# Attention beside a feed-forward network: one head in four forms its scores once, and a transfer turns its probabilities

## The chip, the cores and the metric

One core of one Trainium2 chip. The time is device microseconds of one execution of the whole program; the comparison is between medians of several runs.

## The reference, cut to what matters

`x` is 2048 × 448, there are 16 heads of 28 columns, and the sequence is cut into 4 segments of 512. Within a segment each head attends causally; between segments a linear memory is carried. A feed-forward network runs on the same `x`, and a gate mixes both.

```python
g = sigmoid((x * gate_w).sum(-1, keepdims=True))
# attention, per segment s and head:
logits = einsum("bhqd,bhkd->bhqk", qs, ks) * scale + mask      # causal, 512 x 512
a_dot  = einsum("bhqk,bhkd->bhqd", softmax(logits), vs)
a_mem  = (phi(qs) @ M) / (phi(qs) @ z + 1e-6)                   # memory of earlier segments
o      = sigmoid(beta) * a_mem + (1 - sigmoid(beta)) * a_dot
M, z   = M + phi(ks)^T vs, z + phi(ks) summed
a = concat(o) @ wo
b = silu(x @ w1) @ w2                                           # 448 -> 1792 -> 448
out = g * a + (1 - g) * b
```

## The kernel before, in words

All products run in 16-bit halves: a number is split into a high half and the low half that is left, and a product is the sum of three products of halves. The high half is a copy on ScalarE (ACT), the low half a subtract on VectorE (DVE) or GpSimd (POOL).

The program has three stages. **Projections** (`project`): the features `xT`, the weights `wqs`, `wks`, `wvs`, and from them q, k and v of all segments, which go to DRAM (`q_scr`, `k_scr`, `v_scr`), and the memory terms. `xquarter` (L769) splits the first segment's features in four pieces on DVE (L783, L784), and `weight` (L811) splits the weights (L822; for wq and wk on DVE or POOL, whichever the planner finds free first). `size` (L387) takes largest magnitudes, `scales` (L413 to L431) makes powers of two from them; its TensorE transpose (L417) waits for `most`.

**Attention, with the first FFN pass between.** The 64 heads are taken in 16 groups of four, t = 0 to 15. For each group `maxima(t)` loads q and k into one of four buffers (`ring`), forms all causal scores with queries on partitions (L668; the first block of the four heads shares one bank, which L664 first fills with the mask), and takes row maxima (L673, L678, with the mask tile `mk` added). The maxima go through a small transpose (L686) and two steps (L688, L692) to DRAM (`m_scr`) and come back as two more rows of q. `attention(t)` then forms the scores a second time, now with keys on partitions and the maximum as part of the product (L1219, contraction over 86 rows), in three banks: 512 columns, 384 + 128, 256. ACT takes the exponentials into `pf` (L1224); POOL clears the triangle on the diagonal blocks (L1227, L1230); ACT writes the high half into `phl` (L1236), POOL the low half in three pieces (L1240). With keys on partitions, `phl` is at once the left operand of the product with v (PV, L1253: 20 small products for a head), and DVE adds up its two halves (L1261). Around it run the FFN: the first product (L563, `xh` × `wa`), tanh and the halves (L1098 to L1104), the second product (L1121). Each segment's 16-bit features `xh` are made by `x16` from loads into the two buffers `rawf`.

**The end**: the second FFN pass with the output projection. Its inputs `oT` come by transposing transfers (L588, DMA_TRANSPOSE, 7 blocks of 128 × 128 each).

What sets the order: every instruction group is a task with a priority (`prio`; a head has 10, a group 40), planned durations (`half`, `act`, `dve`, `pool`, `dma`) and buffers. `Sched` plays the program forward and, engine by engine, emits the task that can start first, and among those the one of the least priority. The result is one fixed instruction list for each engine; an engine then waits at each instruction for what it needs. All transfers are issued from SyncE's (SP's) one list. Constants such as `MAXO`, `LOP`, `PVP`, `FLO`, `FHI` shift priorities.

Of the kernel before, what the change touches and what calls it, by code (L numbers as in the profile page):

```python
# [8 lines left out]
F32 = mybir.dt.float32  # L9
# [12 lines left out]
KS = 3 * DH  # L22
# [8 lines left out]
NEG = -1.0e30  # L31
NT = NSEG * NG
NH = NT * 4
NA = 5
COLD = 5.0
# [10 lines left out]
WOT = 59.67  # L46
# [5 lines left out]
HD = 0.15  # L52
# [3 lines left out]
LOP = 11.21  # L56
# [3 lines left out]
MAXO = 66.73  # L60
# [9 lines left out]
VC = -7.68  # L70
OT1 = 8.22
XS = 6.38
QS = -4.77
KS1 = 0.43
# [7 lines left out]
PRICE = 34.19  # L82
PVRUNS = [((1, 0), 1)]
PVP = 44.58
FLO = -16.6
FHI = 688.88
WOP = 89.36
# [27 lines left out]
class Sched:  # L115
# [6 lines left out]
    def __init__(self):  # L122
        self.free = {e: 1.0 for e in self.HOP}
        self.cand = {e: [] for e in self.HOP}
        self.count = 0
        self.port = {"DVE": 0.0, "POOL": 0.0}
        self.tail = 1.0
# [116 lines left out]
def infini_mix(ctx: ExitStack, tc: tile.TileContext, x, wq, wk, wv, wo, beta, w1, w2, out):  # L244
# [226 lines left out]
    def others(s, prio, bds, own, t_own, t_gh):  # L471
# [15 lines left out]
        def scores():  # L487
# [3 lines left out]
            nc.vector.reciprocal(lift[:, s:s + 1], es[:, s:s + 1])  # L491
            nc.vector.tensor_scalar(lift[:, s:s + 1], lift[:, s:s + 1], LIFT, 2.0 ** 29, op0=OP.mult, op1=OP.min)
# [140 lines left out]
    cring("mx", [128, 4, TB], F32, 2, base)  # L633
    cring("mhl2", [16, 2, 128], F16, 1, base)
# [9 lines left out]
    def maxima(t, o):  # L644
# [9 lines left out]
        RDONE[:] = RS[t] = rs  # L654
        reds = []
        plan = [(0, [0, 1, 2, 3]), (1, [0, 1]), (1, [2, 3])] + [(i, [h]) for h in range(4) for i in (2, 3)]
        for q, (i, hs) in enumerate(plan):
# [4 lines left out]
            def go(i=i, hs=hs, ps=ps, n=n):  # L662
                if i == 0:
                    nc.tensor.matmul(ps.v, identb, maskb[:, None, :].to_broadcast([128, 4, 128]), start=True,  # L664
                                     stop=False, skip_group_check=True)
                for j, hh in enumerate(hs):
                    u = j * n
                    nc.tensor.matmul(ps.v[:, u:u + n], rg.v[:KS, 0, hh, i * 128:(i + 1) * 128], rg.v[:KS, 1, hh, :n],  # L668
                                     start=(i > 0), stop=(i > 0 or j == 3), skip_group_check=(i == 0))

            def red(i=i, hs=hs, ps=ps, n=n):
                if i == 0:
                    nc.vector.tensor_reduce(mx.v[:, :, 0], ps.v.rearrange("p (h n) -> p h n", h=4), axis=AX.X,  # L673
                                            op=OP.max)
                    return
# [4 lines left out]
            m = pe((half(512) if i == 0 else []) + half(n, len(hs)), go, *rs, *MKS, takes=[ps], uses=[rg], prio=p0)  # L680
# [5 lines left out]
        f0 = pe(half(128), lambda: nc.tensor.transpose(pt.v[:16, :128], mx.v.rearrange("p h i -> p (h i)"), ident), *reds,  # L686
                takes=[pt], uses=[mx], prio=p0)
        f1 = dve(128, lambda: nc.vector.tensor_scalar(pt.v[:16, :128], pt.v[:16, :128], lift[:16, s:s + 1], None,  # L688
                                                      op0=OP.subtract), f0, EREADY[s], uses=[pt], prio=p0)
        f3 = act(128, lambda: nc.scalar.activation(mh.v[:, 0], pt.v[:16, :128], AF.Copy, scale=1.0 / TALL), f1, takes=[mh],  # L690
                 uses=[pt], prio=p0)
        f4 = dve(128, lambda: nc.vector.scalar_tensor_tensor(mh.v[:, 1], pt.v[:16, :128], 1.0 / TALL, mh.v[:, 0],  # L692
                                                             op0=OP.mult, op1=OP.subtract), f3, uses=[pt, mh], prio=p0)
        d1 = dma(16e3, lambda: start(mscr[t].rearrange("z h i n -> (h i) z n"), mh.v), f4, uses=[mh], prio=p0)
        dm = dma(16e3, lambda: start(rg.v[KS:KS + 2, 0], mscr[t].rearrange("z h i n -> z h (i n)")), d1, uses=[rg],
# [3 lines left out]
    def project():  # L699
# [110 lines left out]

        def weight(name, src, prio, places):  # L811
            n = W[name].shape[2]
            for c, (b, first, v) in enumerate(places):
# [16 lines left out]
                WS[name][c] = [hi, dve(n, lambda lo=lo: lo(nc.vector), hi, **k) if name == "v" else either(n, lo, hi, **k)]  # L830
# [243 lines left out]
    TH, GF, PA = (tiles(fp, n, [128, L], F32, 2) for n in ("th", "gf", "pa"))  # L1074
# [68 lines left out]
    def spare(s, p0, m):  # L1143
        th, gf, g = Buf(TH), Buf(GF), Buf(GTR)
        if s not in SP:
# [4 lines left out]
        e2 = dve(L, lambda: nc.vector.scalar_tensor_tensor(gf.v, th.v, 1.0, h.v, op0=OP.add, op1=OP.mult), e1,  # L1150
                 port=True, takes=[gf], uses=[h, th], prio=p0)
# [257 lines left out]
```

## Time and profile before

| | us |
|---|---|
| median of 3 runs | 558.12 (557.57 to 558.83) |
| the profiled execution | 557.23 |
| its span (first to last instruction) | 555.5 |
| TensorE busy | 541.9 |
| VectorE busy | 413.6 |
| ScalarE busy | 399.7 |
| GpSimd busy | 365.2 |

In the profile, a group is a line of the kernel with its engine, operation and tile names (out<-in), so `L1224 ACT ACTIVATE pf<-sc,es` is the exponential. Its columns are the busy time of all, the mean of one in ns, and the idle time of the engine just before them with what ended it. TensorE's weight loads have a row of their own (PEld) and run beside the products. `SPq` is SyncE's list of transfers: its times are those of the issue, not of the data.

### The profile page before, as it was taken

The numbers are of one execution on the slowest core, as the hardware profiler recorded it, in microseconds if no ns is written. First come the engines' busy times: TensorE is split into PE (matmuls) and PEld (weight loads), VectorE is DVE, ScalarE is ACT, GpSimd is POOL, SyncE is SP. The second block draws the span as 40 slices with busy tenths as digits, with TensorE's granted clock in tenths as the row PEclk, the third lists the DMA queues.
The fourth block names the chain that finished last, engine by engine and source line by source line (L and its number), as shares of the span: only waits on it lengthen the run. The fifth ranks groups of instructions, "written<-read, shape, count | busy, mean of one in ns | idle before, by whom it ended". The sixth has DMA issues, their size and how long they took to land.

```text
span 555.5 us, 11580 instructions
## 1 busy us (share of the span) xinstructions
PE 541.9 (98%) x4007; PEld 340.2 (61%) x4007; DVE 413.6 (74%) x1076; ACT 399.7 (72%) x695; POOL 365.2 (66%) x520
## 2 busy tenths in 40 slices
PE   8799999999999999999999999999999999999997
PEld 5588888888844555555656545565556555555544
DVE  6997998788789966789656888857997228745463
ACT  6467988876656878899778978878998897403140
POOL 5813648637320777999899979998999996212220
PEclk9899999999999999999999999999999999999999
DMA  8479888986775445423344235357302213689972
GB/s 293 153 241 217 229 220 242 224 213 188 216 211 163 130 136 176 122 74 79 108 118 127 68 88 155 108 139 180 90 19 70 69 50 94 226 208 222 251 183 83
DMA packets 91497, 85.87 MB, mean 155 GB/s; under 512 B 55432, under 2 KB 79112, under 8 KB 91440
## 3 DMA queue, kind: packets, MB, share of 16 engines
q1 hardware_dynamic: 91440, 85.15, 55.6%
q8 instruction: 31, 0.51, 0.4%
q14 instruction: 26, 0.21, 0.1%
HBM read 52.60 MB, written 26.09 MB: 142 GB/s over the span
## 4 chain that ended last, share of the span: by engine, by line
PE 84%; POOL 5%; DVE 4%; ACT 3%; DMA 2%; issue 2%; DVEq 0%; POOLq 0%; ACTq 0%
PE mm L563 32%; PE mm L1121 22%; PE sc L563 11%; PE sc L668 5%; PE sc L1219 5%; PE cc L1253 5%; POOL phl L1240 3%; DMA rawf<-in_x_dram 1%; ACT pf L1224 1%; PE cc L973 1%; ACT phl L1236 1%; DVE sizes L387 1%; PE cc L936 1%; DMA xraw<-in_x_dram 1%; PE cc L974 1%
## 5 line engine op out<-in xcount | busy, mean ns | idle before, releaser
L1240 POOL TENSOR_TENSOR phl<-pf,phl 128x384 f16<-128x384 f32 (+1 forms) x192 | 189.2, 1004 | 14.9 <-ACT phl L1236 14.8
L1121 PE MATMUL mm<-wb,ghl 128*128 128x448 f16 (+1 forms) x684 | 148.2, 349 | 0.0
L563 PE MATMUL mm<-xh,wa 128*128 128x512 f16 x572 | 140.3, 379 | 0.0
L1224 ACT ACTIVATE pf<-sc,es 128x512 f32<-128x512 f32 (+1 forms) x192 | 109.6, 620 | 15.7 <-PE sc L1219 12.6
L678 DVE CUSTOM_DVE_ANT_0 sc<-sc,mk 128x384 f32<-128x384 f32 (+1 forms) x192 | 104.6, 572 | 18.0 <-PE sc L668 16.6
L1121 PEld LDWEIGHTS <-ghl 128*128 128x128 f16 x684 | 64.7, 97 | 51.7 <-issue 1.0
L1236 ACT ACTIVATE phl<-pf 128x1280 f16<-128x1280 f32 x64 | 81.4, 1274 | 12.4 <-POOL pf L1230 12.3
L563 PEld LDWEIGHTS <-wa 128*128 128x128 f16 x572 | 53.6, 97 | 53.8 <-issue 0.3
L1219 PE MATMUL sc<-ring 86*128 86x512 f16 (+3 forms) x256 | 58.3, 299 | 2.2 <-ACT pf L1224 1.8
L668 PE MATMUL sc<-ring 84*128 84x128 f16 (+3 forms) x256 | 56.1, 299 | 0.5 <-ACT pf L1224 0.5
L1253 PEld LDWEIGHTS <-phl 128*128 128x128 f16 x1280 | 41.9, 96 | 8.8
L574 POOL TENSOR_TENSOR ol<-ol,ml 128x448 f32<-128x448 f32 x12 | 13.6, 1133 | 51.1 <-DMA ol<-o_scr 42.0
L563 PE MATMUL mm<-xT,wqs 128*128 128x512 f32 x176 | 47.2, 406 | 0.0
L563 PE MATMUL mm<-xT,wks 128*128 128x512 f32 x176 | 45.9, 400 | 0.0
L1098 ACT ACTIVATE th<-mm,ths 128x512 f32<-128x512 f32 x52 | 35.5, 689 | 13.3 <-PE mm L563 13.2
L1253 PE MATMUL cc<-vg,phl 128*128 128x29 f16 (+1 forms) x1280 | 43.6, 182 | 0.0
L1261 DVE TENSOR_REDUCE oraw<-cc 128x116 f32<-128x232 f32 x64 | 25.1, 393 | 23.3 <-PE cc L1253 23.1
L563 PE MATMUL sc<-wvs,xT 128*128 128x450 f32 x176 | 40.4, 373 | 1.0 <-DVE wvs L822 1.0
L1219 PEld LDWEIGHTS <-ring 86*128 86x128 f16 x256 | 24.5, 97 | 26.3 <-issue 3.5
L1227 POOL TENSOR_SCALAR_AFFINE_SELECT pf<-pf 128x128 f32<-128x128 f32 x64 | 20.9, 326 | 27.7 <-ACT pf L1224 25.3
L1104 DVE SCALAR_TENSOR_TENSOR ghl<-mm,ghl 128x512 f16<-128x512 f32 x52 | 35.1, 680 | 5.2 <-ACT ghl L1102 5.1
L1100 DVE SCALAR_TENSOR_TENSOR mm<-th,mm 128x512 f32<-128x512 f32 x52 | 35.4, 691 | 4.1 <-ACT th L1098 4.0
(162 smaller groups left out, 912.1 us busy)
## 6 DMA issues: line engine op xcount, KB each, us to landing
rawf<-in_w_dram SPq DMA_DIRECT2D x26, 256.0 KB
rawf<-in_w_dram SPq DMA_DIRECT2D x28, 224.0 KB
xraw<-in_x_dram SPq DMA_DIRECT2D x16, 256.0 KB
rawf<-in_x_dram SPq DMA_DIRECT2D x16, 256.0 KB
v_scr<-vt SPq DMA_DIRECT2D x16, 232.0 KB
vg<-v_scr SPq DMA_DIRECT2D x16, 232.0 KB
q_scr<-stg SPq DMA_DIRECT2D x16, 224.0 KB
k_scr<-stg SPq DMA_DIRECT2D x16, 224.0 KB
```

The source lines that it names most:

```text
L563: nc.tensor.matmul(ps(), *p[i], start=(i == 0), stop=(i == n - 1))
L668: nc.tensor.matmul(ps.v[:, u:u + n], rg.v[:KS, 0, hh, i * 128:(i + 1) * 128], rg.v[:KS, 1, hh, :n], start=(i > 0), stop=(i > 0 or j == 3), ...
L678: nc.vector.tensor_tensor_reduce(r, r, MK[:, L - n:], 1.0, NEG, OP.add, OP.max, mx.v[:, hh, i:i + 1])
L1098: e1 = sact(L, lambda ps=ps, th=th: nc.scalar.activation(th.v, ps.v, AF.Tanh, scale=ths[:, s:s + 1]), m, takes=[th], uses=[ps], prio=p0)
L1100: e2 = dve(L, lambda ps=ps, th=th: nc.vector.scalar_tensor_tensor(ps.v, th.v, 1.0, ps.v, op0=OP.add, op1=OP.mult), e1, uses=[ps, th], prio=p0)
L1104: e4 = dve(L, lambda ps=ps, g=g: nc.vector.scalar_tensor_tensor(g.v[:, 1], ps.v, DOWN, g.v[:, 0], op0=OP.mult, op1=OP.subtract), e3, uses= ...
L1121: nc.tensor.matmul(ps.v[:, lo:hi], g.v[:, y, sl], w.v[:, z, lo:hi], start=(j == 0 and i == 0), stop=(j == len(fs) - 1 and i == 2))
L1219: nc.tensor.matmul(ps.v[:, e:e + w], rg.v[:KK, 1, hh, j * 128:(j + 1) * 128], rg.v[:KK, 0, hh, j * 128:], start=True, stop=True)
L1224: ex.append(sact(e, lambda b=b, ps=ps, pf=pf, e=e: nc.scalar.activation(pf.v[:, b, :e], ps.v[:, :e], AF.Exp, scale=es[:, s:s + 1]), m, *ex ...
L1236: hi = copy(1280, lambda hl=hl, flat=flat: nc.scalar.activation(hl.v[:, 0], flat(), AF.Copy), *mk, takes=[hl], uses=[pf], prio=p0 + 2)
L1240: low = pool(w - u, lambda hl=hl, flat=flat, u=u, w=w: nc.gpsimd.tensor_sub(hl.v[:, 1, u:w], flat()[:, u:w], hl.v[:, 0, u:w]), low, uses=[ ...
L1253: nc.tensor.matmul(p[:, i, :2 - z], hl.v[:, z, u:u + 128], vg.v[:, j, hh, :2 - z], start=(z == zs[0] and i == 0), stop=(z == zs[-1] and j ...
```

## The change

For groups 1 to 15 the last head is "turned" (`TURNED`). Its scores are formed once, with queries on partitions (4 products, contraction over 84 rows), in three banks: block 3 (512 columns), blocks 2 and 0 (384 + 128), block 1 (256). DVE adds the mask and takes the row maximum, and four one-column operations make the exponential's bias. ACT takes four exponentials with that bias and then the high half, POOL the low half. The probabilities now have queries on partitions, so a transposing transfer turns both halves, 20 blocks of 128 × 128, from `phl` back into the memory of `pf`, and PV reads them from there. `maxima` forms and sends three heads' maxima instead of four for these groups, and the two selects on POOL are not needed for the turned head.

Besides, `pf` has four buffers instead of three, and `gf` goes (its values overwrite `hsum`). In the projections, the low halves of wq and wk also wait for the low halves of the first segment's features (`XLO`). Some fifteen priority constants have other values.

```diff
+NPF = 4
+NPH = 3
+TURNED = [0] + [1] * 15
+TQ = 31.32
+TPV = 38.99
+TD = 3.4
+TDLAT = 4.0
...
-FHI = 688.88
+FHI = 674.33
...
+            nc.vector.tensor_scalar(lift[:, NSEG + s:NSEG + s + 1], es[:, s:s + 1], -1.0, None, op0=OP.mult)
...
-        plan = [(0, [0, 1, 2, 3]), (1, [0, 1]), (1, [2, 3])] + [(i, [h]) for h in range(4) for i in (2, 3)]
+        plan = [(0, list(range(k)))] + [(1, list(range(h, min(h + 2, k)))) for h in range(0, k, 2)]
+        plan += [(i, [h]) for h in range(k) for i in (2, 3)]
...
-                WS[name][c] = [hi, dve(n, lambda lo=lo: lo(nc.vector), hi, **k) if name == "v" else either(n, lo, hi, **k)]
+                WS[name][c] = [hi, dve(n, lambda lo=lo: lo(nc.vector), hi, **k) if name == "v" else either(n, lo, hi, *XLO, **k)]
...
+        XLO.extend(XC[0, tb][1] for tb in range(TB))
...
+    def turned(hh, p0, rg, rs, vg, dv, s):
+        pf, hl, mn = Buf(C["pf"]), Buf(C["phl"]), Buf(C["mn"])
...
+        pq = p0 - TQ
+        for blocks in ((3,), (2, 0), (1,)):
+            ps = Buf(BK["sc"])
+            at = list(zip(blocks, (0, 384)))
...
+                    nc.tensor.matmul(ps.v[:, u:u + n], rg.v[:KS, 0, hh, i * 128:(i + 1) * 128], rg.v[:KS, 1, hh, :n],
+                                     start=True, stop=True)
...
+                    nc.vector.tensor_tensor_reduce(r, r, MK[:, L - n:], 1.0, NEG, OP.add, OP.max, mn.v[:, 0, i:i + 1])
...
+                    nc.vector.tensor_scalar(mn.v[:, 1, i:i + 1], mn.v[:, 0, i:i + 1], lift[:, s:s + 1],
+                                            lift[:, NSEG + s:NSEG + s + 1], op0=OP.subtract, op1=OP.mult)
...
+                    nc.scalar.activation(flat()[:, OFF[i]:OFF[i] + n], ps.v[:, u:u + n], AF.Exp, bias=mn.v[:, 1, i:i + 1],
+                                         scale=es[:, s:s + 1])
...
+        tp = sch.add("SP", TD, lambda: nc.sync.dma_start_transpose(back(), hl.v.rearrange("p z n -> p (z n)")), [low],
+                     uses=[pf, hl], prio=pq, lat=TDLAT)
...
+                        nc.tensor.matmul(p[:, i, :2 - z], v[:, 10 * z + OFF[i] // 128 + j], vg.v[:, j, hh, :2 - z],
+                                         start=(z == 1 and i == 0), stop=(z == 0 and j == i), skip_group_check=True)
```

The order at three places. TensorE at the start of the projections, first before the change; L417 transposes `most`, and `wqs` and `wks` are the split weights:

```order
L563 MATMUL sc<-wvs,xT_101 128x450 x33
L563 MATMUL mm<-xT_101,wqs 128x512 x6
L417 MATMUL cc<-ident,most 2x128
L563 MATMUL mm<-xT_101,wqs 128x512 x5
L563 MATMUL mm<-xT_101,wks 128x512 x3
L426 LDWEIGHTS oneb
L426 MATMUL cc<-diag_120,oneb 128x2
```

The same place after the change (line numbers are the new kernel's):

```order
L572 MATMUL sc<-wvs,xT_101 128x450 x33
L572 MATMUL mm<-xT_101,wqs 128x512 x9
L425 MATMUL cc<-ident,most 2x128
L572 MATMUL mm<-xT_101,wqs 128x512 x5
L572 MATMUL mm<-xT_101,wks 128x512 x3
L434 MATMUL cc<-diag_120,oneb 128x2
```

Nine products with wq stand ahead of the transpose of `most` instead of six. SP's list where the first turned head's transfer stands, first before the change; `rawf<-in_x_dram` are the loads of segment 1's features, `m_scr` and `ring<-m_scr` the maxima's way out and back:

```order
L321 DMA rawf<-in_x_dram 128x512
L321 DMA vg<-v_scr 128x4x232
L321 DMA o_scr<-ob 128x4x112
L321 DMA rawf<-in_x_dram 128x512 x2
L321 DMA m_scr<-mhl_2881 16x2x128
L321 DMA p_scr<-pa 128x448
L321 DMA ring_734<-q_scr 56x2048
L321 DMA ring_2144<-m_scr 2x2048
```

The same place after the change:

```order
L329 DMA rawf<-in_x_dram 128x512
L329 DMA vg<-v_scr 128x4x232
L1262 DMA_TRANSPOSE pf<-phl 128x20x128
L329 DMA rawf<-in_x_dram 128x512 x2
L329 DMA p_scr<-pa 128x448
L329 DMA o_scr<-ob 128x4x112
L329 DMA m_scr<-mhl_2915 12x2x128
L329 DMA p_scr<-pa 128x448
L329 DMA ring_733<-q_scr 56x2048
L329 DMA p_scr<-pa 128x448
L329 DMA ring_2148<-m_scr 2x1536
```

The transfer stands ahead of two of the loads, of the output's write and of the maxima's write. VectorE where a group's last head takes its maxima, first before the change (ISA rows are the masked maximum and its read):

```order
L678 ISA sc_2994,mx<-sc_2994,mk 128x384
L678 ISA mx 128x1
L1261 TENSOR_REDUCE oraw<-cc_3004 128x116
L678 ISA sc_3047,mx<-sc_3047,mk 128x512
L678 ISA mx 128x1
L673 TENSOR_REDUCE mx<-sc_3067 128x4
```

After the change, a turned head on VectorE, with `mn` its maxima and biases:

```order
L1239 ISA sc_3190,mn<-sc_3190,mk 128x512
L1239 ISA mn 128x1
L1241 TENSOR_SCALAR mn<-mn,lift 128x1
L524 SCALAR_TENSOR_TENSOR xh_2150<-rawf,up,xh_2150 64x512
L1239 ISA sc_3194,mn<-sc_3194,mk 128x384
L1239 ISA mn 128x1
L1239 ISA sc_3194,mn<-sc_3194,mk 128x128
L1239 ISA mn 128x1
L1241 TENSOR_SCALAR mn<-mn,lift 128x1 x2
```

Four maxima with their reads and four one-column operations for the bias stand there now, where two maxima, their reads and a quarter of the group's shared reduction stood.

More of the change, by code (lines that the diff above doesn't have):

```diff
@@ L663, in go @@
                 if i == 0:
[L664 removed]
+                    nc.tensor.matmul(ps.v[:, :k * 128], identb, maskb[:, None, :].to_broadcast([128, k, 128]), start=True,
                                      stop=False, skip_group_check=True)
@@ L1197, in attention, with fin, go @@
+    def fin(hh, ps, last, orw, fins, p0):
+        def go():
+            p = ps.v[:, :TB * 58].rearrange("p (i t e) -> p i e t", i=TB, t=2)
+            nc.vector.tensor_reduce(orw.v[:, hh], p, axis=AX.X, op=OP.add)
+        return dve(232, go, last, *fins[:1], takes=[] if fins else [orw], uses=[ps, orw], prio=p0 + PVP)
     def attention(t):
```

119 lines of the change are left out of this document (81 added, 38 removed).

## The prediction

> **What bounds the kernel now.** I read the page first, then the busy time by stage, then the chain of waits in order of time, then the groups with shapes kept apart. The page, from top to bottom: span, TensorE, and the chain that ended last.
>
> ```profile
> span 555.5 us, 11580 instructions
> ...
> PE 541.9 (98%) x4007; PEld 340.2 (61%) x4007; DVE 413.6 (74%) x1076; ACT 399.7 (72%) x695; POOL 365.2 (66%) x520
> ...
> PE 84%; POOL 5%; DVE 4%; ACT 3%; DMA 2%; issue 2%; DVEq 0%; POOLq 0%; ACTq 0%
> ```
>
> TensorE is busy for 541.9 of 555.5 us and carries 84% of the chain. By stage (columns: stretch, its length, then busy time and instructions of PE, PEld, DVE, ACT, POOL, granted clock, DMA share, GB/s):
>
> ```profile
> 0.00:20.00 20.00, 14.35 (x55) 9.14 (x56) 15.02 (x32) 13.16 (x24) 13.67 (x33) 0.98 0.71 250
> 20.00:168.00 148.00, 147.49 (x774) 118.36 (x775) 128.60 (x344) 108.80 (x231) 71.09 (x114) 0.99 0.81 217
> 168.00:452.00 284.00, 280.34 (x2591) 160.99 (x2589) 211.34 (x600) 242.02 (x384) 249.38 (x341) 1.00 0.39 108
> 452.00:555.50 103.50, 99.71 (x592) 51.76 (x589) 58.67 (x104) 35.68 (x58) 31.10 (x34) 1.00 0.66 174
> ```
>
> TensorE's visible idle time is 5.65 us in the first 20 us, 0.51 in the rest of the projections, 3.66 in the attention stage (168 to 452, where the turned heads will lie) and 3.79 after it. In the attention stage GpSimd is busy for 249.38 of 284 us (88%) and ScalarE for 242.02 (85%): both are near enough to the bound to matter. One piece of the chain shows what a matmul really takes when they follow each other closely:
>
> ```profile
> 155.07 13.83 PE mm L563 x64
> ```
>
> 64 products of 512 columns in 13.83 us are 0.216 us each, 0.422 ns a column.
>
> **The change, part by part.** The groups with the durations for the sum (busy us, then mean ns of one):
>
> ```profile
> L1240 POOL TENSOR_TENSOR phl<-pf,phl 128x384 f16<-128x384 f32 x128 | 116.9, 922 | 14.9 <-ACT phl L1236 14.8
> L1224 ACT ACTIVATE pf<-sc,es 128x512 f32<-128x512 f32 x128 | 84.1, 690 | 14.9 <-PE sc L1219 12.0 <-POOL phl L1240 1.0 <-POOL pf L1227 0.6
> L1236 ACT ACTIVATE phl<-pf 128x1280 f16<-128x1280 f32 x64 | 81.4, 1274 | 12.4 <-POOL pf L1230 12.3
> L1240 POOL TENSOR_TENSOR phl<-pf,phl 128x512 f16<-128x512 f32 x64 | 74.8, 1170 | 0.0
> L678 DVE CUSTOM_DVE_ANT_0 sc<-sc,mk 128x512 f32<-128x512 f32 x64 | 45.5, 711 | 2.1 <-PE sc L668 2.0
> L1230 POOL TENSOR_SCALAR_AFFINE_SELECT pf<-pf 128x384 f32<-128x384 f32 x64 | 33.8, 528 | 0.2
> L1224 ACT ACTIVATE pf<-sc,es 128x256 f32<-128x256 f32 x64 | 30.7, 480 | 0.8 <-PE sc L1219 0.6
> L678 DVE CUSTOM_DVE_ANT_0 sc<-sc,mk 128x256 f32<-128x256 f32 x64 | 27.5, 429 | 4.8 <-PE sc L668 3.6
> L678 DVE DVE_READ_ACCUMULATOR2_ANT mx<- 128x1 f32 x192 | 26.7, 139 | 0.0
> L1227 POOL TENSOR_SCALAR_AFFINE_SELECT pf<-pf 128x128 f32<-128x128 f32 x64 | 20.9, 326 | 27.7 <-ACT pf L1224 25.3 <-PE sc L668 1.9 <-PE mm L563 0.4
> L1219 PE MATMUL sc<-ring 86*128 86x128 f16 x64 | 13.9, 217 | 0.0
> L664 PE MATMUL sc<-maskb,identb 128*128 128x512 bf16 x16 | 6.1, 379 | 1.0 <-ACT pf L1224 0.9
> L517 POOL TENSOR_SCALAR rawf<-rawf,up 128x512 f32<-128x512 f32 x3 | 4.7, 1572 | 0.0
> L518 POOL TENSOR_TENSOR xh<-rawf,xh 128x512 f16<-128x512 f32 x2 | 2.3, 1160 | 0.2
> ```
>
> *TensorE, the term that counts.* A turned head forms its scores once. Gone are 512+384+256+128 = 1280 columns (L1219) per head, and 128 of the 512 columns of the group's mask product (L664). The duration rows give (379 − 217)/384 = 0.422 ns a column, the same as the chain. So 1408 columns are 0.594 us, and 15 heads 8.9 us. The PV products stay 20 per head. As TensorE is the bound of that stage, I count all of it: **−8.9 us**. From below, if the products removed had stood where TensorE waited anyway, it is 0 (first rival).
>
> *GpSimd.* Two selects go, 0.326 + 0.528 = 0.854 us, times 15 = 12.8 us. The order shows two low halves of FFN weights coming over from VectorE, each a scale and a subtract (1.57 + 1.16 = 2.7), so 5.5 back. 249.4 − 12.8 + 5.5 = 242 us of a stage then 275 long: 88% as before. No gain by itself.
>
> *VectorE.* Per turned head one more maximum over 128 columns (711 to 429 for half: 141 ns per 128, so 0.29) with its accumulator read, 0.14, and four one-column tensor_scalar, which the row of an equal shape puts at 0.19 each:
>
> ```profile
> 31.33 0.19 DVE L446 TENSOR_SCALAR upw<-up,own 128x1 f32<-128x1 f32 x1
> ```
>
> That is 1.2 us a head, 18 in all; 211 + 18 = 229 of 275 us, 83%: hidden behind TensorE. If this cover failed, at most those 18 us would show.
>
> *ScalarE.* Three exponentials (690 + 690 + 480 = 1.86 us) become four: 512, 384, 256 and 128 columns, 690 + 585 + 480 + 375 = 2.13 on the line through the two rows. The bias from a tile of its own has no row; I take it as free. 0.27 us, times 15 = 4.1: 246 of 275 us, 89%. Hidden, with less room than any other engine.
>
> *The transfer.* No row shows a transpose of this size. The nearest is L588's, 7 blocks of 128×128 against 20 here. First all of them, with minimum, median and maximum ns of their issue; then SP's queue; then the DMA in three stretches of 1 us after that issue:
>
> ```profile
>   L588 SPq DMA_TRANSPOSE oT<-oh x16: 1220/1222/2151, 362.1 to 542.3; - x16
> ```
>
> ```profile
> 538.12 5.41 SPq L588 DMA_TRANSPOSE oT<-oh  x2
> ```
>
> ```profile
> 539.00:540.00 1.00, 1.00 (x8) 0.51 (x6) 0.23 (x1) 0.00 (x0) 0.52 (x1) 1.00 0.72 143
> 540.00:541.00 1.00, 1.00 (x7) 0.54 (x6) 0.00 (x0) 0.35 (x1) 0.61 (x1) 1.00 0.46 86
> 541.00:542.00 1.00, 1.00 (x7) 0.51 (x6) 0.65 (x2) 0.31 (x1) 0.00 (x0) 1.00 0.00 0
> ```
>
> The first of that pair is issued from 538.12 to 539.34, and its 229 KB move by 541: 143 + 86 GB/s over 1 us each, with the 16 engines busy for 0.72 + 0.46 = 1.18 us, 194 GB/s. For 20 blocks: issue 1.22 × 20/7 = 3.5 us, 655 KB at 194 GB/s = 3.4 us, which overlaps the issue, and 1.7 us from the end of the issue to landing: 5.2 us. Bounds: 2.9 us (no dearer than 7 blocks) and 2.9 × 20/7 = 8.3. The DMA share of the stage rises from 0.39 by 15 × 3.4/275 = 0.19: room enough.
>
> Who waits for it: the turned head's PV. From its last score the chain is maximum, read and bias (0.43 + 0.14 + 0.19), exponential 0.48, high half 1.27, low half 0.92 + 1.17 + 0.92, transfer 5.2: 10.7 us. In the new order I counted the columns TensorE has between a turned head's last score and its PV: at 0.422 ns they are 15 to 17 us for 14 of the 15 groups, so 4 us and more to spare, and 7.7 us for the second turned head: 3 us short. That place is just ahead of the first FFN product of segment 1, where the new order runs out of FFN products: 6.3 us of attention alone, with 10 heads' PV done before that product against 8 in the old order. What TensorE waits for there today:
>
> ```profile
> PE sc L1219 <- ACT pf L1224: 1.8, 2, 1.4
> ```
>
> ```profile
> 216.93 3.83 DMA rawf<-in_x_dram
> ```
>
> 1.8 us, both times around the late load of segment 1's features. So I add **+1.5 us**, between 0 (the new wait takes the old one's place) and +5 (3 us at this PV and 2 more behind ScalarE).
>
> [...]
>
> Behind the transfer on SP's queue stand the write of the group before's output, the row maxima's write and read-back, and the loads of q and k, which `maxima` plans seven heads ahead of their use. Only the maxima's pair is planned close to its use (second rival).
>
> *The start.* The low halves of wq and wk now wait for the features' low halves. VectorE, then GpSimd, then TensorE:
>
> ```profile
> 10.26 0.29 DVE L784 TENSOR_TENSOR xT<-xraw,xT 64x128 fp32r<-64x128 f32 x1
> 10.58 0.56 DVE L783 TENSOR_TENSOR xT<-xraw,xT 128x384 fp32r<-128x384 f32 x1
> 11.17 1.27 DVE L784 TENSOR_TENSOR xT<-xraw,xT 64x128 fp32r<-64x128 f32 x1
> 12.47 1.55 DVE L783 TENSOR_TENSOR xT<-xraw,xT 128x384 fp32r<-128x384 f32 x1
> 14.05 1.27 DVE L784 TENSOR_TENSOR xT<-xraw,xT 64x128 fp32r<-64x128 f32 x1
> ...
> 19.77 0.15 DVE L413 TENSOR_REDUCE most<-sizes 128x2 f32<-128x8 f32 x1
> ```
>
> ```profile
> 10.91 5.56 POOL L822 TENSOR_TENSOR wqs<-raw,wqs 128x512 fp32r<-128x512 f32 x4 [3.38 <-ACT wqs L819]
> 16.45 4.95 POOL L822 TENSOR_TENSOR wks<-wa,wks 128x512 fp32r<-128x512 f32 x4
> ```
>
> ```profile
> 14.79 1.53 PE L563 MATMUL mm<-xT,wqs 128*128 128x512 f32 x6
> 19.98 0.37 PE L417 MATMUL cc<-ident,most 128*2 128x128 f32 x1 [3.65 <-DVE most L413]
> ```
>
> From the moment GpSimd's subtracts begin (10.91), VectorE's take 1.27, 1.55 and 1.27 instead of 0.29, 0.56 and 0.29. With GpSimd held back they end 2.95 us earlier, and so does the chain to `most`, for which TensorE waits 3.65 us. GpSimd then starts near 12.4, and its third piece ends at 12.4 + 3 × 1.39 = 16.6; the order puts 9 products ahead of L417 instead of 6, so L417 comes near 17.4 with three products more done: 2.6 + 3 × 0.23 = 3.3 us ahead. The low halves of wk end 1.5 us later, which takes some of it back. **−2.5 us**, between −1 and −3.5.
>
> *The other constants and buffers* only reorder. Between start and end TensorE visibly waits 0.51 + 3.66 = 4.2 us, which bounds what order can win; I count 0, with −3 to +1.5.
>
> **The sum.** The profiled execution took 557.23 us, its span 555.5. 557.23 − 8.9 + 1.5 − 2.5 = 547.3. The runs' median, 558.12, lies 0.9 above the profiled execution; put on that scale, **548.2 us**.
>
> **The rivals.** *1. ScalarE paces the attention stage.* Its load rises by 4.1 us while TensorE's falls; if the stage ends on it, the stage stays 284 us and only the start is won: 558.12 − 2.5 = 555.6. For it: the waits in the stage name ACT (the 1.8 us above). Against: 85% busy, and TensorE 98.7%. [...] 8%.
>
> *2. Slower: SP's queue holds up the row maxima.* The transfer waits at the head of SP's queue for GpSimd's last subtract and then holds it 3.5 us; behind it are the write and read-back of the next group's maxima, without which its scores can't start. The gain is 548.2 against 558.1, 9.9 us, so 0.66 us of waiting per group uses it up; at 1 us per group 548.2 + 15 = 563. For it: one queue, in order, and each such transfer costs as much queue time as three 7-block ones. Against: TensorE has FFN products to put in between. 8%.
>
> *3. The start and the first heads give less*: the projections are held by VectorE (128.6 of 148 us), so the start wins 1, and the gap before segment 1 costs 5: 558.1 − 8.9 − 1 + 5 = 553.2. 12%.
>
> *4. Better:* the start −3.5, no new gap, 3 us of waits closed by the order: 558.1 − 8.9 − 3.5 − 3 = 542.7. 10%.
>
> **Chances.** The forecast (545 to 551) 60%, the rivals 8, 8, 12 and 10%, 2% beyond. About 0.2% (1.1 us) is what a measurement here can tell from no change. Rivals 1, 3, 4 and the forecast are faster by more than that; part of 1 is not. Faster 0.88, the same 0.04, slower 0.08. The range: 543.0 (rival 4) to 554.5 (rival 3 with 1.3 us lost by the order).
>
> **What would show it.** Right: TensorE's busy time near 533, no wait of TensorE on the transfer but at the second group, L417 near 17.4, the transfer's issue near 3.5 us. Wrong: waits of the scores on the read-back of the maxima in every group (rival 2), or a stage still 284 us long with ScalarE above 90% (rival 1).

## The result, and the profile after

| | before | after |
|---|---|---|
| median, us | 557.85 (557.32 to 558.83, 4 runs) | 572.75 (570.47 to 573.06, 4 runs) |
| profiled execution, us | 557.23 | 572.6 |
| its span, us | 555.5 | 570.9 |
| mean granted TensorE clock | 0.997 | 0.975 |

The ratio is 1.0264, with a 95% interval from 1.0247 to 1.028: **14.9 us slower**, where 9.9 faster was forecast. The page of the changed kernel (its lines are numbered 8 to 90 higher: L563 is now L572, L1219 is L1309, L417 is L425):

```profile
span 570.9 us, 11580 instructions
...
PE 546.3 (96%) x3947; PEld 338.4 (59%) x3947; DVE 428.7 (75%) x1168; ACT 407.3 (71%) x710; POOL 362.8 (64%) x494
...
PE 64%; DVE 17%; ACT 5%; DMA 5%; issue 3%; POOL 3%; SPq 1%; DVEq 0%; POOLq 0%; ACTq 0%
```

TensorE's share of the chain falls from 84 to 64%, VectorE's rises from 4 to 17%. TensorE is visibly idle for 570.9 − 546.3 = 24.6 us instead of 13.6, 11.0 more. It also ran slower: at a mean clock of 0.975 the span holds 570.9 × 0.025 = 14.3 us of clock that was not granted, before 555.5 × 0.003 = 1.7, so 12.6 more. With the 8.9 us of columns removed that makes 11.0 + 12.6 − 8.9 = 14.7, against 15.4 by the spans: the columns are gone as forecast, and 24 us of idle and slow time came. Where, the stretches show (cut at the end of the last head's high half, 459.4 and 476.0; before, then after):

```profile
20.00:168.00 148.00, 147.49 (x774) 118.36 (x775) 128.60 (x344) 108.80 (x231) 71.09 (x114) 0.99 0.81 217
168.00:459.40 291.40, 287.74 (x2644) 164.69 (x2642) 214.01 (x605) 249.42 (x395) 256.71 (x352) 1.00 0.38 107
459.40:555.52 96.12, 92.31 (x538) 48.06 (x536) 56.00 (x98) 28.28 (x47) 23.78 (x23) 1.00 0.70 183
```

```profile
20.00:168.00 148.00, 146.26 (x761) 117.32 (x762) 126.24 (x348) 106.70 (x229) 71.27 (x114) 0.98 0.80 215
168.00:217.60 49.60, 49.19 (x394) 27.41 (x392) 39.52 (x108) 41.32 (x68) 31.25 (x41) 1.00 0.59 162
217.60:238.20 20.60, 15.53 (x120) 7.81 (x118) 14.30 (x45) 13.89 (x23) 17.92 (x22) 0.59 0.53 136
238.20:476.00 237.80, 231.96 (x2126) 130.54 (x2124) 178.80 (x550) 206.11 (x327) 205.81 (x267) 0.99 0.53 130
476.00:570.86 94.86, 88.11 (x499) 45.55 (x497) 54.97 (x93) 26.16 (x43) 21.82 (x20) 0.99 0.63 181
```

The attention stage takes 308 us instead of 291.4; the rest is as long as it was. The longest gap lies where the prediction had put its +1.5 us, ahead of segment 1's first FFN product. On TensorE:

```profile
217.63 0.77 PE L682 MATMUL sc<-ring 84*128 84x384 f16 x2
220.85 1.26 PE L1309 MATMUL sc<-ring 86*128 86x512 f16 x4 [2.45 <-ACT pf L1247]
...
234.47 1.49 PE L572 MATMUL mm<-xh,wa 128*128 128x512 f16 x3
```

and on VectorE, with a turned head's maxima:

```profile
214.32 0.73 DVE L1239 CUSTOM_DVE_ANT_0 sc<-sc,mk 128x512 f32<-128x512 f32 x1
214.97 0.14 DVE L1239 DVE_READ_ACCUMULATOR2_ANT mn<- 128x1 f32 x1
215.14 0.27 DVE L1241 TENSOR_SCALAR mn<-mn,lift 128x1 f32<-128x1 f32 x1
215.33 0.39 DVE L1280 TENSOR_REDUCE oraw<-cc 128x116 f32<-128x232 f32 x1
...
217.12 2.37 DVE L524 SCALAR_TENSOR_TENSOR xh<-rawf,up,xh 128x512 f16<-128x512 f32 x2 [0.16 <-ACT pf L1247]
219.41 0.42 DVE L1239 CUSTOM_DVE_ANT_0 sc<-sc,mk 128x256 f32<-128x256 f32 x1
219.75 0.14 DVE L1239 DVE_READ_ACCUMULATOR2_ANT mn<- 128x1 f32 x1
219.93 0.27 DVE L1241 TENSOR_SCALAR mn<-mn,lift 128x1 f32<-128x1 f32 x1
220.11 0.39 DVE L1280 TENSOR_REDUCE oraw<-cc 128x116 f32<-128x232 f32 x1
```

TensorE has run out of work at 218.4; its next scores wait for a score bank that a turned head still holds. That head's last exponential waits for its scale, and the scale stands on VectorE behind two FFN subtracts. In the stretch from 217.6 to 238.2, TensorE is idle for 20.60 − 15.53 = 5.1 us and has a clock of 0.59. The first product of xh comes at 234.47, before at 220.60.

### The profile page after: what moved, and what is told of

Its sections match the earlier page's. It is cut to its first block, busy times and chain, and to the rows that moved or that the text cites. A ratio compares the mean times of both kernels' runs of the same rounds, so it can differ in the third digit from the quotient of the medians.

```text
span 570.9 us, 11580 instructions
## 1 busy us (share of the span) xinstructions
PE 546.3 (96%) x3947; PEld 338.4 (59%) x3947; DVE 428.7 (75%) x1168; ACT 407.3 (71%) x710; POOL 362.8 (64%) x494
## 4 chain that ended last, share of the span: by engine, by line
PE 64%; DVE 17%; ACT 5%; DMA 5%; issue 3%; POOL 3%; SPq 1%; DVEq 0%; POOLq 0%; ACTq 0%
PE mm L572 27%; PE mm L1138 15%; PE sc L572 9%; PE sc L1309 3%; PE sc L682 3%; DVE sc L692 3%; PE cc L1343 3%; DVE sc L1239 2%; ACT pf L1314 1%; DVE ghl L1121 1%; DMA rawf<-in_x_dram 1%; DMA ol<-o_scr 1%; DVE mm L1117 1%; DMA rawf<-in_w_dram 1%; DVE mn L1241 1%
## 5 line engine op out<-in xcount | busy, mean ns | idle before, releaser
L1330 POOL TENSOR_TENSOR phl<-pf,phl 128x384 f16<-128x384 f32 x147 | 148.3, 1025 | 15.0 <-ACT phl L1326 14.7
L572 PE MATMUL mm<-xh,wa 128*128 128x512 f16 x572 | 144.4, 387 | 1.9 <-DVE ghl L1121 1.4
L692 DVE CUSTOM_DVE_ANT_0 sc<-sc,mk 128x256 f32<-128x256 f32 (+2 forms) x147 | 81.1, 567 | 24.1 <-PE sc L682 21.7
L1314 ACT ACTIVATE pf<-sc,es 128x512 f32<-128x512 f32 x147 | 84.5, 623 | 8.6 <-PE sc L1309 7.6
L572 PEld LDWEIGHTS <-wa 128*128 128x128 f16 x572 | 54.5, 99 | 58.6 <-issue 7.8
L1326 ACT ACTIVATE phl<-pf 128x1280 f16<-128x1280 f32 x49 | 62.7, 1280 | 7.9 <-POOL pf L1320 6.0
L1257 POOL TENSOR_TENSOR phl<-pf,phl 128x384 f16<-128x384 f32 (+1 forms) x45 | 44.9, 1009 | 24.3 <-ACT phl L1254 24.3
L1309 PE MATMUL sc<-ring 86*128 86x512 f16 x196 | 45.0, 309 | 5.3 <-ACT pf L1247 2.5
L682 PE MATMUL sc<-ring 84*128 84x384 f16 (+2 forms) x196 | 48.9, 309 | 1.0 <-ACT pf L1314 0.6
L1247 ACT ACTIVATE pf<-sc,mn,es 128x512 f32<-128x512 f32 (+3 forms) x60 | 34.5, 615 | 19.3 <-DVE mn L1241 19.1
L572 PE MATMUL mm<-xT,wqs 128*128 128x512 f32 x176 | 47.7, 408 | 0.0
L1115 ACT ACTIVATE th<-mm,ths 128x512 f32<-128x512 f32 x52 | 35.5, 701 | 16.7 <-PE mm L572 16.5
L572 PE MATMUL mm<-xT,wks 128*128 128x512 f32 x176 | 46.7, 400 | 0.0
L583 POOL TENSOR_TENSOR ol<-ol,ml 128x448 f32<-128x448 f32 x12 | 13.6, 1133 | 50.7 <-DMA ol<-o_scr 24.7
L572 PE MATMUL sc<-wvs,xT 128*128 128x450 f32 x176 | 40.7, 374 | 0.8 <-DVE wvs L838 0.7
L1343 PEld LDWEIGHTS <-phl 128*128 128x128 f16 x980 | 33.0, 97 | 13.5 <-issue 3.9
L589 ACT ACTIVATE oh<-ol,os 128x448 f16<-128x448 f32 x16 | 10.6, 665 | 42.0 <-POOL ol L583 40.8
```

The costliest lines, as they stand in the source:

```text
L572: nc.tensor.matmul(ps(), *p[i], start=(i == 0), stop=(i == n - 1))
L692: nc.vector.tensor_tensor_reduce(r, r, MK[:, L - n:], 1.0, NEG, OP.add, OP.max, mx.v[:, hh, i:i + 1])
L1257: low = pool(w - u, lambda u=u, w=w: nc.gpsimd.tensor_sub(hl.v[:, 1, u:w], flat()[:, u:w], hl.v[:, 0, u:w]), low, uses=[pf, hl], prio=pq + ...
L1309: nc.tensor.matmul(ps.v[:, e:e + w], rg.v[:KK, 1, hh, j * 128:(j + 1) * 128], rg.v[:KK, 0, hh, j * 128:], start=True, stop=True)
L1314: ex.append(sact(e, lambda b=b, ps=ps, pf=pf, e=e: nc.scalar.activation(pf.v[:, 512 * b:512 * b + e], ps.v[:, :e], AF.Exp, scale=es[:, s:s ...
L1326: hi = copy(1280, lambda hl=hl, flat=flat: nc.scalar.activation(hl.v[:, 0], flat(), AF.Copy), *mk, takes=[hl], uses=[pf], prio=p0 + 2)
```

## The experiments

The theory at first: a gap at the turned heads ahead of segment 1 and the low clock behind it (theory 1). Rivals: the transfers hold up SP's queue (theory 2, the prediction's second rival), and the new constants make a bad order (theory 3).

**Constants, heads and transfer apart.** No head turned:

```diff
-TURNED = [0] + [1] * 15
+TURNED = [0] * 16
```

> No head is turned; the changed constants, buffers and start order stay. Theory 1 (the loss is a TensorE gap ahead of segment 1's first FFN product, where turned heads are on a longer chain and no FFN product is left, and the clock that falls to half behind it): no such gap, so 555 to 560 us, granted clock 0.99 or more. Theory 2 (the transfers hold up SP's queue, a little in every group): the same, 555 to 560. Theory 3 (the new constants order the work badly, turned heads or not): 565 us or more, with half-rate windows again, as the 8.9 us of removed columns come back.

**575.57 us** (571.80 to 576.35), ratio 1.0296 (1.0257 to 1.0334). Without one turned head the kernel is as slow as with 15. What TensorE waits for is elsewhere, above all at the end of the attention stage (5.9 us in two waits, at 473 and 485 us; the wait for `most` stands in the kernel before too):

```profile
PE mm L572 <- DVE ghl L1121: 5.9, 2, 4.3
PE cc L425 <- DVE most L421: 3.1, 1, 3.1
PE sc L1309 <- ACT pf L1314: 2.9, 2, 2.0
```

Theory 3 was right here and theory 1 wrong. The other way round, turned heads with the old values of the twelve constants:

```diff
-LOP = 7.29
+LOP = 11.21
...
-WOP = 94.92
+WOP = 89.36
```

> 15 turned heads with the planner's twelve constants of the kernel before. Theory 1: the gap belongs to the turned heads and not to the constants, so 565 to 578 us with a half-rate stretch of several windows somewhere before 250 us. Theory 2: 565 to 575 us, without a need for such a stretch. Theory 3: the old constants give the predicted time, 546 to 552 us, clock 0.99.

**590.25 us** (586.62 to 591.03), ratio 1.0568 (1.0533 to 1.0604): worse than any theory had it, and theory 3's forecast for this run (546 to 552) failed too. The constants that suit plain heads don't suit turned ones. Then the first turned heads left out:

```diff
-TURNED = [0] + [1] * 15
+TURNED = [0] * 4 + [1] * 12
```

> The first turned head moves from the second group to the fifth, so that none lies ahead of segment 1's first FFN product; 12 heads stay turned and 12 x 0.594 = 7.1 us of columns stay removed. Theory 1: the gap and its half-rate windows go, 548 to 556 us. Theory 2: 12 of 15 transfers stay and so does 12/15 of their cost, 566 to 571 us. Theory 3: 565 us or more.

**573.37 us** (571.15 to 573.93), ratio 1.0271 (1.0247 to 1.0295). The long gap at 220 is gone (0.88 us idle from 220 to 240, clock 1.00), and another has opened: 4.9 us idle and a clock of 0.77 from 460 to 480. A gap at that one place is not what the loss hangs on. The transfer:

```diff
-    dma_start_transpose(back(), hl.v.rearrange("p z n -> p (z n)"))
+    dma_start_transpose(back()[:, :1], hl.v.rearrange("p z n -> p (z n)")[:, :128])
...
-            v = back()
+            v = hl.v.rearrange("p z (j n) -> p (z j) n", n=128)
```

> Every order stays as it is; the transfer moves 1 block instead of 20, and the PV products read the unturned halves and wait for no transfer (so the attention's values are not computed). Theory 1, with the gap made by the longer chain on ScalarE and VectorE: 568 to 573 us, half-rate windows stay. Theory 1, with the gap made by the loads that stand behind the transfer on SP's queue: 555 to 562 us. Theory 2: 550 to 560 us. Theory 3: 570 us or more.

The transfers' issue, in the changed kernel and then here:

```profile
L1262 SPq DMA_TRANSPOSE pf<-phl x15: 3009/3116/3671, 206.1 to 464.1; - x15
```

```profile
L1262 SPq DMA_TRANSPOSE pf<-phl x15: 1105/1212/2692, 206.9 to 462.7; - x15
```

**571.19 us** (569.28 to 573.28), ratio 1.024 (1.0206 to 1.0274): 1.6 us less than the change by the medians, and the two ranges overlap. 15 × 1.904 = 28.6 us less of SP's queue, and PV products that need no transfer, change the time by no more than these runs can tell. Theory 2 falls.

**The clock.** Useless work where TensorE runs dry:

```diff
+AGAIN = {(3, 3, 1): 11, (3, 2, 2): 4, (3, 3, 2): 6, (4, 1, 0): 3, (4, 1, 2): 4, (4, 2, 0): 4}
...
-                for j, hh in enumerate(hs):
-                    u = j * n
+                for j, hh in enumerate(hs * AGAIN.get((t, i, hs[0]), 1)):
+                    u = j % len(hs) * n
```

> Same order; 28 of the maxima's score products (groups 4 and 5, between 217 and 231 us) are repeated in place, 5.0 us of useless TensorE work at full clock, at the places where TensorE runs dry. If idle time is what lowers the granted clock, and the low clock is what makes the gap so long: the five half-rate windows from 221 to 238 us become two or none, the first product of xh of segment 1 comes 3 to 6 us earlier than 234.5, and the time is 566 to 570 us. If the low clock comes from something else (load, power): the windows stay and the time is 573 to 578. If TensorE is only waiting for ScalarE and GpSimd there, and the clock costs nothing: the windows go, but the time stays at 571 to 574.

**576.02 us** (572.25 to 578.69), ratio 1.0316 (1.0265 to 1.0367). The gap now:

```profile
220.00:222.00 2.00, 1.74 (x27) 1.13 (x27) 0.76 (x4) 1.91 (x4) 2.00 (x3) 1.00 0.38 140
...
226.00:228.00 2.00, 1.38 (x12) 0.93 (x12) 0.82 (x3) 2.00 (x4) 2.00 (x4) 0.89 1.12 222
228.00:230.00 2.00, 1.41 (x19) 1.21 (x20) 1.04 (x5) 0.27 (x3) 2.00 (x4) 0.50 0.77 207
```

The filling keeps the clock full until 227.5, and half rate lasts some 7 us instead of 17. But the first product of xh comes at 233.59, no more than 0.9 us earlier, and the time is 3 us longer by the medians (the ranges overlap): nearest to the third branch, which had no loss. With the useless work in TensorE's gaps the clock reads 1.00 from 221 to 226, where the change has 0.50 from 221.1 on, and yet no time is won: there the low clock costs little. GpSimd is busy for 2.00 of 2 us in all three rows, and in the changed kernel's own chain of waits it holds 7.4 of the 8.7 us from 222.2 to 230.9: its work sets the length of the gap there.

**How much one constant does.** The kernel before, and nothing but:

```diff
-LOP = 11.21
+LOP = 7.29
```

> The kernel before, with one of the twelve planner's constants of the change: LOP, the lag of GpSimd's low halves in the planner's ranking, 7.29 for 11.21. No head is turned. Theory 3, sharpened (the order before is a fragile optimum, and almost any shift of a constant opens TensorE gaps and half-rate windows elsewhere): 566 to 576 us with two or more half-rate windows after 100 us. Rival (the constants reorder only what has slack; the loss in the run without turned heads came from the changed buffers or the start): 556 to 560 us.

**571.06 us** (570.70 to 571.30), ratio 1.0231 (1.0212 to 1.025). One number in the planner's ranking costs 12.9 us (0.0231 × 558), as much as the whole change less 2. TensorE waits for low halves of GpSimd, most of it at 480 to 483 us, and after the stage, at 526 and 531, for VectorE; the wait for `most` was there before.

```profile
PE cc L1253 <- POOL phl L1240: 3.9, 4, 1.7
PE cc L417 <- DVE most L413: 3.6, 1, 3.6
PE mm L1121 <- DVE y L1334: 1.9, 2, 1.5
```

**Orders that fit.** Constants set anew (24 or 25 of them, where the expectation counts 23), for 15 turned heads and, as a control, for none:

```diff
-LOP = 7.29
-TQ = 31.32
-TPV = 38.99
+LOP = 9.81
+TQ = 35.64
+TPV = 27.58
...
```

> 15 turned heads with 23 of the planner's constants set anew for them. If the turned heads are worth their 8.9 us wherever the order keeps TensorE fed: 546 to 556 us, at most three half-rate windows. If the longer chain of a turned head (maximum, four scales, exponentials with a bias, transfer) costs TensorE time in any order: 565 us or more, with waits on L1247 or L1241 in most groups.

> No turned head, with the planner's constants set anew for that in the same manner, and the change's other code as it is: the control to the run before it. If order is what counts and turning is worth 8.9 us: 555 to 562 us, 6 to 10 us above that run. If turning is worth nothing once the order suits: within 3 us of that run. If turning costs: 5 us or more below it.

**564.71 us** (563.62 to 566.45), ratio 1.0121 (1.0094 to 1.0148), with turned heads; **557.63** (554.98 to 558.82), ratio 0.9974 (0.9952 to 0.9995), without. An order that fits is worth 8 us to the change and 18 to the run without turned heads, and with both fitted turning costs 7. Neither branch of the first expectation is met (564.7 lies between), and TensorE has no wait on L1247 or L1241 in most groups.

So what does a turned head cost that the order doesn't know? The planner gives the maximum of block 3 `dve(512 + 70)`, that is 0.07 + 0.00104 × 582 = 0.675 us. In the VectorE rows above, maximum, read and scale hold VectorE from 214.32 to 215.33, 1.01 us; block 1, planned at 0.41, from 219.41 to 220.11, 0.70. The missing 0.3 us is the one-column scale and part of the accumulator's read, four times a head. Is VectorE's part on the path? Every scale twice:

```diff
-                for i, u in at:
+                for i, u in at + at:
                     nc.vector.tensor_scalar(mn.v[:, 1, i:i + 1], mn.v[:, 0, i:i + 1], lift[:, s:s + 1],
```

> Each one-column scale of a turned head's maxima is issued twice: 60 instructions more on VectorE, 4 a head, each 0.19 to 0.27 us, nothing else. If VectorE's part of a turned head is hidden behind TensorE, as the prediction had it: 571 to 575 us. If it lies on the path of every turned head (score bank, maximum, scale, exponential, bank free), the time rises by 0.5 to 1 us a head, 8 to 15 us: 580 to 588. If only the gap ahead of segment 1 matters: 573 to 577.

**584.44 us** (584.12 to 585.16), ratio 1.0461 (1.0437 to 1.0486): 11.7 us more, 0.78 a head. The group's busy time, here and in the change:

```profile
L1241 DVE TENSOR_SCALAR mn<-mn,lift 128x1 f32<-128x1 f32 x120 | 28.6, 269 | 2.2
```

```profile
L1241 DVE TENSOR_SCALAR mn<-mn,lift 128x1 f32<-128x1 f32 x60 | 15.0, 270 | 1.1
```

13.6 us more on an engine that was busy for 75% of the span, and 11.7 of them show; TensorE's idle time rises from 24.6 to 582.5 − 545.4 = 37.1 us. VectorE's part of a turned head is on the path of this order. Then a chain that was meant to be lighter:

```diff
-                for i, u in at:
-                    nc.vector.tensor_scalar(mn.v[:, 1, i:i + 1], mn.v[:, 0, i:i + 1], lift[:, s:s + 1],
-                                            lift[:, NSEG + s:NSEG + s + 1], op0=OP.subtract, op1=OP.mult)
+                c = slice(min(blocks), max(blocks) + 1, max(1, max(blocks) - min(blocks)))
+                nc.vector.tensor_scalar(mn.v[:, 1, c], mn.v[:, 0, c], lift[:, s:s + 1],
+                                        lift[:, NSEG + s:NSEG + s + 1], op0=OP.subtract, op1=OP.mult)
```

> The two scales of the pair of blocks become one instruction of two columns: 15 instructions fewer on VectorE, 0.2 us a head. On the path of every head: 15 x 0.2 = 3 us less, 568.5 to 570.5. Hidden: 571.5 to 574.

**574.48 us** (572.37 to 576.97), ratio 1.028 (1.0253 to 1.0308): nothing gained. The trace shows why: the chain did not become lighter.

```profile
L1241 DVE TENSOR_SCALAR mn<-mn,lift 128x2 f32<-128x2 f32 x15 | 8.5, 570 | 0.5
L1241 DVE TENSOR_SCALAR mn<-mn,lift 128x1 f32<-128x1 f32 x30 | 8.2, 273 | 1.1
```

A scale of two columns takes 570 ns in the mean, more than two of one column. The scales together hold VectorE for 16.7 us, against 15.0 in the change: 1.7 us more work, and the median is 1.7 us higher. So this run doesn't say what less work on VectorE would win.

If the order is at fault, one made with the real durations should mend it. The planner is told, first with the change's own constants, then with constants set anew, then with others:

```diff
-            d = dve(w + 70 * (k - 1) + 70 * k, red, m, EREADY[s], *reds[-1:], ...
+            d = dve(w + 70 * (k - 1) + 70 * k + 250 * k, red, m, EREADY[s], *reds[-1:], ...
```

> The change as it is, with its own constants, and only the planner's duration for a turned head's maximum raised by 0.26 us a block. If the missing duration is the cause and the order mends itself once it is told: 556 to 564 us. If constants that suit are needed as well: 568 to 578.

> 15 turned heads; the planner is told 0.26 us more for each block's maximum, accumulator read and scale of a turned head (four a head), which is about what the trace shows, and its constants are set anew for that. If the loss with fitted constants (564.7 us) came from an order made with too short a chain: 556 to 561, and the order as planned is kept. If turned heads cost that much in any order: 563 us or more.

> A second order with 15 turned heads whose planner is told the 0.26 us more a block, with another set of constants. If the missing duration is what made the other orders slow: 555 to 561 us, like the first one told (556.8). If the first was luck of its constants: anywhere from 562 to 580.

And a second order with constants set anew that is not told:

> A second order with 15 turned heads and constants set anew, the planner not told. If the missing duration is what counts: 562 to 568 us, like the first of its kind (564.7), 5 to 9 us above the order that is told. If constants alone decide: 556 to 560, as low as the told ones.

| 15 turned heads | planner not told | planner told |
|---|---|---|
| the change's constants | 572.75 | 578.82, ratio 1.0385 (1.035 to 1.042) |
| constants set anew | 564.71 | **556.79**, ratio 0.9965 (0.9947 to 0.9983) |
| others set anew | 566.49, ratio 1.0134 (1.0106 to 1.0162) | 562.64, ratio 1.0058 (1.0037 to 1.0079) |

Told alone, with constants made for the wrong chain, it is worse. With constants set anew, the told orders are 8 and 4 us better than the untold. That suggests that the missing duration is part of the cause, but doesn't show it: the two told orders differ by 6 us from each other, by constants alone, and the second one's 562.64 us lies in the range that its expectation had given to luck of the constants (562 to 580), 1.6 us above the one given to the duration.

**The start.** In the change the low halves of wq were to wait for the features' low halves. They don't: `XLO` is a dependency in the planner, but the program's waits come from the data that an instruction reads, and this one reads none of the features. GpSimd's first ones in the change:

```profile
11.07 5.57 POOL L838 TENSOR_TENSOR wqs<-raw,wqs 128x512 fp32r<-128x512 f32 x4 [2.12 <-ACT gate L921]
```

They start at 11.07 us, right behind ScalarE and not VectorE, while the last of the features' low halves ends at 15.48 (14.21 + 1.27, below). A real wait:

```diff
                 def lo(e, c=c, v=v):
+                    if name == "q" and c == 0:
+                        e.tensor_copy(held, raw(XT[0].v[:, 6, L - 8:]))
+                        e.tensor_copy(held[REM:], raw(XT[0].v[REM:128, NC, L - 8:]))
                     e.tensor_sub(W[name][:, 4 + c], v(), raw(W[name][:, c]))
```

> The change as it is, but GpSimd now really waits, ahead of its first low half of wq, for the features' last low half (two small copies that read it). If GpSimd's running is what slows VectorE's subtracts there (the prediction's price, -2.5 us): they take 0.29 and 0.56 us again instead of 1.27 and 1.55, the line that puts the scale together comes near 17.4 instead of 20.14 us, and the time is 569 to 571. Rival (holding GpSimd back only moves the loss to the low halves of wq and wk, on which the first products wait): the line comes earlier, but the projections' products wait more and the time stays at 572 to 575.

VectorE and TensorE at that place, in the change:

```profile
12.64 1.54 DVE L797 TENSOR_TENSOR xT<-xraw,xT 128x384 fp32r<-128x384 f32 x1
14.21 1.27 DVE L798 TENSOR_TENSOR xT<-xraw,xT 64x128 fp32r<-64x128 f32 x1
...
19.92 0.16 DVE L421 TENSOR_REDUCE most<-sizes 128x2 f32<-128x8 f32 x1
```

```profile
20.14 0.37 PE L425 MATMUL cc<-ident,most 128*2 128x128 f32 x1 [3.12 <-DVE most L421]
```

and with the wait:

```profile
11.82 0.56 DVE L797 TENSOR_TENSOR xT<-xraw,xT 128x384 fp32r<-128x384 f32 x1
12.41 0.29 DVE L798 TENSOR_TENSOR xT<-xraw,xT 64x128 fp32r<-64x128 f32 x1
...
17.16 0.15 DVE L421 TENSOR_REDUCE most<-sizes 128x2 f32<-128x8 f32 x1
```

```profile
17.55 0.28 PE L425 MATMUL cc<-ident,most 128*2 128x128 f32 x1
```

**567.36 us** (565.90 to 569.17), ratio 1.0163 (1.013 to 1.0196): 5.4 us less than the change. The mechanism is as predicted (0.56 and 0.29 us; 17.55 for 17.4), and GpSimd's first subtract now starts at 13.14 us, behind the copies that read the features. The gain is larger than the 2.5 us. With the wait gone TensorE stays at full rate behind it: the granted clock from 20 to 24 us is 0.61 in the change and 1.00 here, worth 1.6 us; and from 156 to 160 us it is 1.00 instead of 0.56 and 0.59. The same wait in the two best orders:

> The 15 turned heads in the order made with their real durations (556.8 us), plus GpSimd's real wait at the start. The line that puts the scale together comes near 17.5 us; if the start's gain carries to this order: 551 to 555 us. If it only shifts a wait (the projections or the loads of the features for segment 1 set the pace later): 556 to 558.

> The control without turned heads (557.6 us) with the same real wait at the start. If the start's gain is independent of the heads: 552 to 556 us, and the distance to the run with turned heads stays 1 us or so. If turned heads are what makes room for it: 556 to 558.

**555.54 us** (554.34 to 560.13), ratio 0.9958 (0.9938 to 0.9979), with 15 turned heads; **555.75** (554.96 to 556.32), ratio 0.9952 (0.9935 to 0.9969), without. Here the wait is worth 1.3 and 1.9 us by the medians, less than the spread between runs of one kernel. These two are the fastest versions found, both faster than the kernel before by 0.4 to 0.5%, and no different from each other. Their pages, turned and plain:

```profile
span 552.7 us, 11568 instructions
...
PE 534.2 (97%) x3947; PEld 335.1 (61%) x3947; DVE 436.4 (79%) x1182; ACT 406.4 (74%) x710; POOL 341.1 (62%) x481
```

```profile
span 554.0 us, 11550 instructions
...
PE 541.9 (98%) x4007; PEld 338.9 (61%) x4007; DVE 428.4 (77%) x1105; ACT 401.1 (72%) x695; POOL 335.1 (60%) x494
```

At the same clock (0.997), TensorE has 541.9 − 534.2 = 7.7 us less to do with turned heads, and is idle for 18.5 us instead of 12.1, 6.4 more. What turning saves on TensorE, TensorE then waits.

## Why the prediction was wrong

**The step that failed** is "The other constants and buffers only reorder. Between start and end TensorE visibly waits 0.51 + 3.66 = 4.2 us, which bounds what order can win; I count 0, with −3 to +1.5." The 4.2 us bound what an order can win, and nothing bounded what it can lose. Measured, the change without its turned heads costs 16.5 us (0.0296 × 557.6), and one of its constants alone 12.9. All the forecast's cases, the slower one too, priced single waits and took the rest of the new order to be as tight as the old.

Point by point:

- *TensorE −8.9.* Right as work. Its busy time was said to come near 533: it is 534.2 at a full clock in the best order, 7.7 below the plain one. In the change it reads 546.3, the low clock's 12.6 us included.
- *VectorE +18 us, "hidden behind TensorE".* The size is near (428.7 − 413.6 = 15.1), the cover is not. The one-column scale takes 0.27 us and not 0.19; the profile before had a nearer row, with two operands from tiles as here:

```profile
L490 DVE TENSOR_SCALAR es<-top,es 128x1 f32<-128x1 f32 x4 | 1.1, 274 | 0.1
```

  But what counts is that the scale stands between a score bank and its release: doubling it costs 0.78 us a head. The fallback ("at most those 18 us would show") was the better guide.
- *ScalarE +4.1, the bias free.* The bias is not free: the four exponentials take 775 + 670 + 564 + 451 ns = 2.46 us a head instead of the 2.13 forecast, and ScalarE is busy for 407.3 − 399.7 = 7.6 us more. That it stays below 90% of the stage (rival 1) holds even so: (41.32 + 13.89 + 206.11) / 308 = 85%.
- *The gap ahead of segment 1, +1.5, at most +5.* Right place, but another mechanism and another size. The wait was to be at the second turned head's PV, for its transfer; TensorE sits idle before none of the turned heads' PV products (L1272). Ahead of this stage's scores it waits 2.45 us for a score bank, which is held through the turned head's scale on VectorE, and the first product of xh comes 13.9 us later than before. Yet this gap is a symptom: with no turned head near it the time stayed, and the gap was elsewhere.
- *The start, −2.5.* Price right, and never paid out: the wait is in the planner only. The order of instructions showed 9 products ahead of that line, which was taken for the gain; the operands of one GpSimd instruction would have shown that nothing waits for the features.
- *The transfer* (3.5 us of issue forecast, 3.1 measured) *and rival 2* (SP's queue): no part in it that the runs can tell, 1.6 us by the medians.

**What is shown, and what is not.** Shown: order alone loses what the change loses. The change's code without a turned head is 16.5 us slower, the same code with other constants is back at 557.63, and one constant alone costs the kernel before 12.9. Shown too: VectorE's part of a turned head is on the path of the change's order (doubled scales, 11.7 us), and in the best orders found turning is worth nothing either way. Not shown: that the 0.3 us a block that the planner doesn't know of make an order slow. Told orders are 8 and 4 us better than untold ones when both have constants set anew, and 6 us worse with the change's own, and constants alone move two told orders by 6. So it stays open how much of the change's own 14.9 us belongs to its constants and how much to the missing duration, and whether a still better order would let the 7.7 us show.

## What to carry to other kernels

In a kernel whose instruction order is planned ahead and whose bound engine is 98% busy, a change of a duration or a constant can make another order; price that first, as a loss that the waits in the profile don't bound, and compare a change only between orders made anew for each side. Give the planner the measured length of whatever holds a shared buffer, the small instructions included, and set its constants anew with it: told alone, this order got worse. When an instruction is merged to save time, look up what the merged one takes. And a dependency in a planner is no wait: look at what the instruction reads.

## What the runs showed of the hardware

- **The clock fell for pieces of about 3.4 us.** In the change, TensorE waits 1.6 us for GpSimd near 153, and then:

```profile
154.00:156.00 2.00, 1.46 (x10) 1.14 (x11) 1.88 (x5) 0.00 (x0) 1.35 (x3) 1.00 0.84 257
156.00:158.00 2.00, 2.00 (x7) 0.72 (x6) 1.58 (x10) 0.00 (x0) 1.00 (x3) 0.56 0.87 254
158.00:160.00 2.00, 2.00 (x7) 0.74 (x6) 1.27 (x9) 0.52 (x1) 0.45 (x1) 0.59 0.28 89
```

  Between 157 and 159 us the clock reads 0.50, so a mean of 0.56 and 0.59 over 2 us each is (0.44 + 0.41) × 2 / 0.5 = 3.4 us at half rate; near 221 it lasted 17 us, five times that (0.50 in every slice of 1 us from 222 to 238), and with the filling 6.8 us, twice that. In the run with doubled scales 1.6 us of waiting at the same place left the clock at 1.00. So a wait of one length stood ahead of a fall in one run and of none in another; what decides it, these runs don't show.
- **VectorE's subtracts took longer beside GpSimd's.** VectorE's subtracts of 0.56 and 0.29 us take 1.54 and 1.27 while GpSimd subtracts, and 0.56 and 0.29 again when it is held back; why, no trace here shows. Of the fifteen scales of two columns, 570 ns in the mean, nine take 0.29 to 0.46 us and six 0.78 to 1.17, all six while GpSimd works on two tensors, whereas none of the 60 scales of one column in the change takes more than 0.275.
- **With more operands from tiles the same operation took longer.** The exponential over 512 columns takes 775 ns with a bias from a tile (L1247) and 693 without (L1314); the one-column scale with two operands from tiles takes 270 ns (274 in the kernel before, L490), where one with a single such operand has 202 (L489) and one with none 154 (L497).

```profile
L1314 ACT ACTIVATE pf<-sc,es 128x512 f32<-128x512 f32 x98 | 64.5, 693 | 8.6 <-PE sc L1309 7.6 <-POOL pf L1317 0.9
...
L1247 ACT ACTIVATE pf<-sc,mn,es 128x512 f32<-128x512 f32 x15 | 11.6, 775 | 9.8 <-DVE mn L1241 9.6
```
